# Holding the loads of partial sums and of rows of x to their place in a step, and making some weight forms a step ahead of a single-row-block step's successor

## The chip, the cores and the metric

The kernel runs on one core of a Trainium2 chip. The metric is the time of one execution on the device in microseconds (us). Before the change the median of three runs is 1437.77 us (1435.68 to 1437.93). The engines are TensorE (PE in the profile, PEld for its weight loads), VectorE (DVE), ScalarE (ACT), GpSimd (POOL) and SyncE (SP). SP does no arithmetic here: it issues DMA transfers, one after the other in the order of its queue. POOL issues DMA transfers too, and adds.

## The reference

An input x of 8 batches, 4224 tokens and 192 channels goes through a causal depthwise convolution of 7 taps (the weights are a softmax per head). Its result, called x again below, enters a token-mixing block:

```
theta = x @ w_theta
zr, zi = x * cos(theta), x * sin(theta)
y = einsum('ts,bsd->btd', w_tok_r, zr) + einsum('ts,bsd->btd', w_tok_i, zi)
u = x + y
out = u + maximum(u @ w_ch, 0)
```

The two matrices w_tok_r and w_tok_i have 4224 x 4224 elements each, so the two token products are nearly all of the work. The output is float32.

## The kernel before, in words

**Tiles.** Batches and channels together make 1536 columns. Output rows are cut into 33 row blocks of 128 tokens, input tokens into 33 chunks of 128. For each chunk a tile z of fp16 holds the products of x with cosine and sine and five sums of them. For the weights there are two staging tiles st (one for w_tok_r, one for w_tok_i), and tiles wt which hold "forms": a form is a block of weights turned into the layout that TensorE wants, or a sum or difference of two of those.

**Steps.** The token product runs in 58 steps. A step takes two row blocks (a pair) and all active chunks, at most 11. It computes a product of 2 x 2 blocks (row blocks by matrices, matrices by channel halves) with seven block products instead of eight, which is why sums of z and of weights are needed. There are 33 row blocks, so every 17th step has a single row block: steps 6, 23, 40 and 57. Such a step has four block products, uses no sums of weights, and is short. A block product over all chunks of a step is called a run below; with 11 chunks a run has 22 matmuls (L536) on accumulators y in PSUM. There are two y tiles at a time. After most runs VectorE (L461, `give`; in the first 17 steps partly ScalarE, L459) adds an accumulator into the step's partial sum pv in SBUF, and the next run on the same accumulator waits until that addition has read it.

**Partial sums.** The 33 chunks are taken in three groups of 11. So each row block is visited several times; between visits its partial sum of 768 KB lies in a DRAM tile `part`. `load_rows` (L425) loads the partial sums of the next step, and the end of `mix` (L549) stores those of this step. On some visits the rows of x themselves are added: `load_x` (L432) loads 384 KB into a tile xr, of which there is one alone, and `add_x` (L439) adds it on GpSimd. In the last visits the output is computed and stored (L585, L590).

**Forms.** `load_w` (L374, four transfers on GpSimd's queue) loads the weights of a step two steps ahead. `turn` (L387) turns a quarter of them on VectorE, and `wsum` (L399) adds or subtracts two forms. A pair step needs four turns, named "11", "21" (from w_tok_r) and "22", "12" (from w_tok_i), and four sums S1 to S4. `w_tasks` says when they are made: during the step before.

**Order.** All events of a step have a time between 0 and 7 (a seventh of the step, which in a pair step is a run). `step_events` collects them, and `mix` writes each into the program ahead of the matmul that is due. On PE, DVE and ACT, and for GpSimd's additions and weight loads, that written order is kept, by `in_order`. For DMA issues on SP no such order was asked for: a scheduler places each as soon as its buffer and data allow by its own estimate, so a load can come to stand well ahead of its event. The six buffers named "big" hold the partial sums pv and the convolution's input windows xw.

**Beside the steps.** While a group of chunks is being started (steps 0 to 5, 17 to 22, 35 to 40) TensorE also does the convolution (L216), transposes and the product with w_theta (L146) of the next step's new chunks. VectorE does four products (L297, two for each chunk) and eight sums (L306) when two new chunks start in the next step; the third sum of a chunk overwrites its x, and therefore waits for the four transfers (L263, on SP) that store that x to DRAM.

## Time and profile before

| quantity | value |
|---|---|
| median of three runs | 1437.77 us |
| the profiled execution | 1437.8 us, of which the span of the profile is 1436.0 us |
| PE busy | 1409.4 us, 98% of the span |
| DVE busy | 973.0 us, 68% |
| POOL busy | 434.3 us, 30% |
| ACT busy | 310.6 us, 22% |
| DMA | 281.99 MB, mean 196 GB/s |

The span is what the profile shows, from the first instruction of the program to the last; 1.8 us of the profiled execution's time lie around it. A line of a timeline gives the start, the length, the engine, the source line, the operation, what it writes and reads, how many instructions were merged, and in square brackets how long the engine was idle before and what ended that. "SPq" is a DMA issue on SP. Steps carry no label in the trace: they are found by counting the 7672 matmuls of L536 in order. A step has 2 matmuls for each chunk and run. By that count step 22 begins at 545.8 us, step 23 at 572.1, step 24 at 586.4, step 39 at 966.2, step 40 at 992.4, step 41 at 1010.3 and step 42 at 1038.4. In step 23 the four runs begin at 572.06, 575.63, 579.21 and 582.78 us, so a run of 22 matmuls takes 3.57 us.

### The profile page before, as it was taken

The page shows a single profiled execution, that of the slowest core. Times are in us where ns is not written, and L with a number is a line of the kernel's source. Part 1 is how long each engine was busy: PE and PEld are TensorE (multiplying, and loading weights), DVE is VectorE, ACT ScalarE, POOL GpSimd, SP SyncE. Part 2 cuts the span into 40 slices and gives each one's busy share as a digit, 9 for nine tenths or more (in the row PEclk, how much of TensorE's full clock was granted, in tenths as well). Part 3 has the DMA queues.
Part 4 walks back from the last instruction along what each step waited for, and adds up shares of the span by engine and source line. Part 5 has one row for each costly group of instructions (what it writes and reads, how often), then busy time and mean ns, then how long its engine had stood idle before and what let it go on. Part 6 is the DMA issues. An engine that isn't in the chain of part 4 may idle for free.

```text
span 1436.0 us, 23771 instructions
## 1 busy us (share of the span) xinstructions
PE 1409.4 (98%) x9829; PEld 889.7 (62%) x9829; DVE 973.0 (68%) x1046; ACT 310.6 (22%) x374; POOL 434.3 (30%) x655
## 2 busy tenths in 40 slices
PE   8889999999999999999999999999999999999997
PEld 5556666666666666666666666666566666666665
DVE  6893554545548787866665657877777677767676
ACT  5851101111124244000000004335100110010133
POOL 8511211111233332532333343233323123213110
PEclk9999999999999999999999999999999999999999
DMA  9975766564799999898899889999999999999894
GB/s 193 234 164 132 147 125 128 100 151 89 147 232 227 231 236 239 209 256 177 232 236 229 229 157 243 231 198 255 248 206 216 215 206 220 203 202 197 166 214 136
DMA packets 272045, 281.99 MB, mean 196 GB/s; under 512 B 106688, under 2 KB 240192, under 8 KB 271936
## 3 DMA queue, kind: packets, MB, share of 16 engines
q0 software_dynamic: 162464, 92.15, 48.8%
q1 hardware_dynamic: 71840, 178.88, 35.4%
q10 hardware_dynamic: 37632, 9.44, 4.5%
q8 instruction: 77, 1.26, 0.4%
q14 instruction: 32, 0.26, 0.1%
HBM read 245.49 MB, written 108.13 MB: 246 GB/s over the span
## 4 chain that ended last, share of the span: by engine, by line
PE 92%; DMA 2%; DVE 2%; ACT 1%; SPq 1%; issue 1%; POOL 0%; DVEq 0%; ACTq 0%; POOLq 0%
PE y L536 84%; PE v L146 5%; PE tp L170 1%; PE pc L216 1%; ACT z L291 1%; DMA xw<-in_x_dram 1%; DMA xw<-xw 1%; SPq L194 1%; DVE pv L461 0%; DVE z L306 0%; DVE pv L585 0%; DMA part<-pv 0%; DMA st<-in_moe_w_tok_r_dram 0%; DMA wsb<-in_weight_dram 0%; DVE wt L399 0%
## 5 line engine op out<-in xcount | busy, mean ns | idle before, releaser
L536 PE MATMUL y<-z,wt 128*128 128x384 f16 x7672 | 1282.4, 326 | 6.4 <-DVE pv L461 5.3
L536 PEld LDWEIGHTS <-wt 128*128 128x128 f16 x7672 | 743.7, 98 | 482.6 <-issue 6.3
L461 DVE TENSOR_TENSOR pv<-y,pv 128x768 f32<-128x768 f32 x317 | 302.5, 954 | 323.9 <-PE y L536 284.0
L387 DVE STREAM_TRANSPOSE wt<-st 128x1408 f16<-128x1408 f16 (+7 forms) x224 | 327.5, 1465 | 51.0 <-PE y L536 38.3
L374 POOL DMA_DIRECT2D st<-in_moe_w_tok_r_dram x232 | 132.3, 578 | 463.5 <-DVE wt L387 451.8
L374 POOL DMA_DIRECT2D st<-in_moe_w_tok_i_dram x232 | 132.4, 579 | 405.0 <-DVE wt L387 396.5
L399 DVE TENSOR_TENSOR wt<-wt 128x1408 f16<-128x1408 f16 (+6 forms) x208 | 173.4, 834 | 40.5 <-PE y L536 38.3
L156 ACT ACTIVATE z<-pc 128x768 f16<-128x768 f32 (+1 forms) x62 | 47.5, 803 | 387.0 <-PE pc L216 378.4
L156 ACT ACTIVATE ub<-pv 128x768 f16<-128x768 f32 x63 | 50.2, 836 | 343.6 <-DVE pv L461 315.9
L459 ACT ACTIVATE pv<-y 128x768 f32<-128x768 f32 x66 | 53.7, 814 | 280.5 <-PE y L536 280.5
L146 PEld LDWEIGHTS <-uT 128*128 128x128 f16 x1056 | 90.6, 98 | 23.8 <-issue 5.9
L439 POOL TENSOR_TENSOR pv<-pv,xr 128x1536 f32<-128x1536 f32 x24 | 74.5, 3103 | 66.2 <-issue 26.7
L203 POOL DMA_DIRECT2D xw<-in_x_dram x132 | 76.3, 587 | 27.1 <-issue 7.0
L585 DVE SCALAR_TENSOR_TENSOR pv<-v,pv 128x768 f32<-128x768 f32 (+1 forms) x67 | 62.8, 942 | 24.9 <-PE v L146 24.5
L306 DVE TENSOR_TENSOR z<-z 128x768 f16<-128x768 f16 x132 | 71.2, 552 | 2.2
L291 ACT ACTIVATE z<-v,half_pi 128x768 f16<-128x768 f32 x66 | 59.6, 903 | 56.4 <-PE v L146 55.7
L156 ACT ACTIVATE uT<-tp 128x1536 f16<-128x1536 f16 (+1 forms) x47 | 56.5, 1208 | 47.3 <-PE tp L170 47.3
L297 DVE TENSOR_TENSOR z<-z 128x1536 f16<-128x1536 f16 (+1 forms) x68 | 60.6, 926 | 4.3 <-ACT z L291 4.2
L146 PE MATMUL v<-wth,uT 128*128 128x192 f16 x528 | 54.4, 246 | 2.7 <-ACT z L291 2.1
L146 PE MATMUL v<-wch,uT 128*128 128x192 f16 x528 | 54.3, 246 | 1.3 <-DVE pv L585 0.7
L291 ACT ACTIVATE z<-v 128x768 f16<-128x768 f32 x66 | 53.2, 806 | 0.0
L216 PE MATMUL pc<-xw,bands 96*64 96x192 f16 x512 | 30.4, 251 | 5.4 <-DMA st<-in_moe_w_tok_r_dram 2.7
(45 smaller groups left out, 144.8 us busy)
## 6 DMA issues: line engine op xcount, KB each, us to landing
part<-pv SPq DMA_DIRECT2D x79, 768.0 KB, 4.3
pv<-part SPq DMA_DIRECT2D x79, 768.0 KB, 6.0
out_dram<-pv SPq DMA_DIRECT2D x65, 384.0 KB, 4.5
st<-in_moe_w_tok_r_dram POOLq DMA_DIRECT2D x136, 176.0 KB, 6.0
st<-in_moe_w_tok_i_dram POOLq DMA_DIRECT2D x136, 176.0 KB, 5.3
xs<-z SPq DMA_DIRECT2D x132, 96.0 KB, 5.1
xw<-in_x_dram POOLq DMA_DIRECT2D x121, 96.0 KB, 6.2
xr<-xs SPq DMA_DIRECT2D x24, 384.0 KB, 4.5
```

The source lines that it names most:

```text
L146: pe(nc.tensor.matmul(v[:, k, b * D : (b + 1) * D], lhsT=tT[:, 3 * k + b + i, :], rhs=w[:, 2 * b + i, :], start=(i == 0), stop=(i == 1),))
L156: act(nc.scalar.activation(out=out, in_=in_, func=AT.Copy))
L203: nc.gpsimd.dma_start(out=self.xw[lo : lo + n, h, :, :], in_=x[:, t0 : t0 + n, :].rearrange("b s d -> s b d"),)
L291: act(nc.scalar.activation(**args))
L306: dve(nc.vector.tensor_tensor(out=z[:, o, :], in0=z[:, a, :], in1=z[:, b, :], op=ALU.subtract))
L374: pool(nc.gpsimd.dma_start(out=st[a * Q : (a + 1) * Q, 0:nb, :, 0:n] .rearrange("i r bt s -> i (r bt) s"), in_=w[self.tbs[0] * P : (self.t ...
L387: dve(nc.vector.transpose(self.w[name][:, 0 : self.n, :, :], self.st[int(name[1])][:, int(name[0]) - 1, :, 0 : self.n * Q] .rearrange("p b ...
L399: dve(nc.vector.tensor_tensor(out=self.w[name][:, 0 : self.n, :, :], in0=self.w[a][:, 0 : self.n, :, :], in1=self.w[b][:, 0 : self.n, :, : ...
L439: ins = pool(nc.gpsimd.tensor_tensor(out=self.pv[i], in0=self.pv[i], in1=self.xr[i], op=ALU.add))
L461: dve(nc.vector.tensor_tensor(out=o, in0=yv, in1=o, op=ALU.add))
L536: pe(nc.tensor.matmul(y[cn][:, q, 0:BH], lhsT=self.w[wn][:, c, :, :].rearrange("p bt i -> p (bt i)"), rhs=chunks[k].z[:, zn, q * BH : (q + ...
L585: dve(nc.vector.scalar_tensor_tensor(out=ub[:, ks, :], in0=v[:, ks, :], scalar=0.0, in1=ub[:, ks, :], op0=ALU.max, op1=ALU.add,))
```

## The change

Three things are changed.

- Every load of partial sums and of rows of x (`load_rows`, `load_x`) now waits for the VectorE instruction that was last written into the program before it. `add_x` did so before.
- For the pair steps that follow a single-row-block step (7, 24 and 41) the forms "11", "21" and S3 are made at the end of the step two ahead (5, 22 and 39) by `early_tasks`; the rest of the forms stays in the single-row-block step (6, 23, 40) at other places.
- In a single-row-block step the two loads of weights for the step two ahead stand at 0.1 and 3.1 instead of 1.3 and 4.3.

```
+    def paced(ins):
+        tc.add_manual_dep(ins.ins, last["dve"].ins.name, SYNC, reason="pace")
+        return ins
...
+            if self.t and not steps[self.t - 1].pair:
+                return [
+                    (0.3, lambda: self.turn("22")), (1.1, lambda: self.wsum("S1")),
+                    (1.9, lambda: self.wsum("S2")), (2.9, lambda: self.turn("12")),
+                    (4.0, lambda: self.wsum("S4")),
+                ]
...
+        def early_tasks(self):
+
+            return [
+                (5.9, lambda: self.turn("11")), (6.3, lambda: self.turn("21")),
+                (6.6, lambda: self.wsum("S3")),
+            ]
...
-                    nc.sync.dma_start(
+                    paced(nc.sync.dma_start(
                         out=pv, in_=part[(self.t // NU - 1) % 2][tb, :, :]
-                    )
+                    ))
...
-            nc.sync.dma_start(
+            paced(nc.sync.dma_start(
                 out=self.xr[i], in_=xs[self.tbs[i] * P : (self.tbs[i] + 1) * P, :]
-            )
+            ))
...
-            tc.add_manual_dep(ins.ins, last["dve"].ins.name, SYNC, reason="pace")
+            paced(ins)
...
-                found.append((1.3 + 3 * (m - 1), lambda m=m: nxt.load_w(m)))
+                at = 1.3 + 3 * (m - 1) if s.pair else (0.1, 3.1)[m - 1]
+                found.append((at, lambda m=m: nxt.load_w(m)))
+            if not steps[t + 1].pair:
+                found += nxt.early_tasks()
```

The order of instructions on PE and ACT is the same in both programs. On DVE it differs at the three places around steps 5, 22 and 39. On SP and POOL, DMA issues change places in many steps; those that matter to a step of the prediction are named there.

## The prediction, made before the changed kernel was run

> **What bounds the kernel now.** I read the busy shares first, then the slices, then who waited for whom on PE from 990 us on, then timelines around the single-row-block steps. The page:

> ```profile
> PE 1409.4 (98%) x9829; PEld 889.7 (62%) x9829; DVE 973.0 (68%) x1046; ACT 310.6 (22%) x374; POOL 434.3 (30%) x655
> ...
> PE   8889999999999999999999999999999999999997
> ...
> q0 software_dynamic: 162464, 92.15, 48.8%
> q1 hardware_dynamic: 71840, 178.88, 35.4%
> ```

> TensorE is idle for 26.6 us of 1436.0, and the change leaves every matmul in place, so only idle time can be won. The slices put most of it in the start (14 us before 99 us) and the end (8 us after 1411 us), where the edits hardly reach. In between PE has no gap from 101 to 1004 us, steps 22 to 24 included; what the middle loses lies around step 40. In the waits of PE from 990 us on the largest row, and the timeline of the place (start, length, engine, line; in brackets idle time and who ended it):

> ```profile
> PE y L536 <- DVE pv L461: 3.5, 4, 1.9
> ```

> ```profile
> 996.97 2.28 POOL L374 DMA_DIRECT2D st<-in_moe_w_tok_r_dram  x4 [7.49 <-DVE wt L387]
> ...
> 1001.53 2.30 SPq L425 DMA_DIRECT2D pv<-part  x3
> ...
> 1013.97 0.95 DVE L461 TENSOR_TENSOR pv<-y,pv 128x768 f32<-128x768 f32 x1
> ...
> 1014.97 3.73 PE L536 MATMUL y<-z,wt 128*128 128x384 f16 x22 [0.90 <-DVE pv L461]
> ...
> 1018.03 1.65 DVE L387 STREAM_TRANSPOSE wt<-st 128x1408 f16<-128x1408 f16 x1 [3.11 <-DMA st<-in_moe_w_tok_r_dram]
> 1019.60 0.92 DVE L461 TENSOR_TENSOR pv<-y,pv 128x768 f32<-128x768 f32 x1
> ...
> 1020.57 24.70 PE L536 MATMUL y<-z,wt 128*128 128x384 f16 x151 [1.86 <-DVE pv L461]
> ```

> Two stalls, 0.90 + 1.86 = 2.76 us. In the first VectorE is merely behind (four forms and sums, and the products of two new chunks, in a short step). In the second it sits 3.11 us for weights issued at 997 us, because five loads of partial sums, two at 997.6 and three at 1001.5, shared the DMA engines with them: these weights took up to 19.2 us to land (the transfers of tile st from 990 to 1030 us), against a median of 6.0 on the page.

> **Part 1, the moved forms.** "11", "21" and S3 leave steps 6, 23 and 40 for steps 5, 22 and 39. VectorE before, at the end of step 22:

> ```profile
> 570.35 0.95 DVE L461 TENSOR_TENSOR pv<-y,pv 128x768 f32<-128x768 f32 x1
> 571.21 1.14 DVE L306 TENSOR_TENSOR z<-z 128x768 f16<-128x768 f16 x2
> 572.27 0.95 DVE L461 TENSOR_TENSOR pv<-y,pv 128x768 f32<-128x768 f32 x1
> 573.14 3.16 DVE L387 STREAM_TRANSPOSE wt<-st 128x1408 f16<-128x1408 f16 x2
> 576.22 0.92 DVE L461 TENSOR_TENSOR pv<-y,pv 128x768 f32<-128x768 f32 x1
> 577.06 0.87 DVE L399 TENSOR_TENSOR wt<-wt 128x1408 f16<-128x1408 f16 x1
> ```

> VectorE has no idle time there, and in the changed program's order both turns and S3 stand ahead of the addition at 572.27, the last of step 22. From starts: two turns 576.22 - 573.14 = 3.08, S3 577.86 - 577.06 = 0.80, together 3.88 us. The addition ends at 577.1. The second run of step 23 needs its accumulator at 575.63, so PE stalls 1.52 us where it had none. In step 39 the same 3.88 us put the addition of 992.64 to 996.5, ending 997.4; step 40's second run, spread out by convolution and transposes, wants it at 996.93: 0.45 us lost. In return VectorE is done in step 40 ahead of step 41's second run (1013.9 against 1014.4 by the same replay): the 0.90 goes. What is late next there: step 40's last sums, which wait for the x stores queued on SP behind the loads for step 41; these now go about 3 us later, behind an addition at 1000.6. In step 5 VectorE has 18 of 25 us free, and three late forms cost nothing; without that cover it would be 1.5 us as in step 22.

> **Part 2, the loads of step 42 and 43** leave step 40 for 1.6 sevenths into steps 41 and 42. The weights issued at 997 us (now about 996, since "21" is turned earlier) then share the engines with two loads of sums instead of five. By the page's rows q0, the weights' queue, moves 92.15 MB in 48.8% of 1436 us, 131 MB a ms, and q1 352: 5.5 us of engine time for 704 KB of weights, 2.2 for a load of sums. All that is in flight from 996.5 comes to some 13 us; VectorE wants the weights at 1013.8. The 3.11 us and the 1.86 us go. Same sum for the old order: 20 us from 997.5, which is the landing seen.

> **Part 3, the loads of step 24.** This is where I expect the price.

> ```profile
> 557.50 1.49 SPq L425 DMA_DIRECT2D pv<-part  x3
> ...
> 581.43 3.10 POOL L439 TENSOR_TENSOR pv<-pv,xr 128x1536 f32<-128x1536 f32 x1 [2.56 <-DVE wt L399]
> ...
> 584.56 0.32 SPq L432 DMA_DIRECT2D xr<-xs  x1
> ...
> 589.38 3.10 POOL L439 TENSOR_TENSOR pv<-pv,xr 128x1536 f32<-128x1536 f32 x1 [2.60 <-DMA xr<-xs]
> ...
> 594.89 0.32 SPq L425 DMA_DIRECT2D pv<-part  x1
> 595.31 0.37 SPq L432 DMA_DIRECT2D xr<-xs  x1
> ```

> Step 24 is the first that adds x. Before, its sums came at 557.5, and the first rows of x had been in their tile since 70 us; even so the second addition of x ended at 592.5, 1.3 us ahead of VectorE's addition of 593.78. Now both sums wait for the first addition of step 23, which ends at 580.5, and the rows of x, third in SP's queue, for S2 at 581.3. GpSimd's queue has the second load of weights ahead of x's addition; it needs "12" (582.8), so the queue is free at 585.2 and does not decide. The second rows need the single tile xr, and SP now has the store of step 23's sum ahead of them, issued by 589: it does not decide either.

> When do the first rows land? Nearest row: the rows issued at 595.31 behind one load of sums, with weights beside, landed 9.0 us on. One more load ahead is 2.2: 581.3 + 11.2 = 592.5. Ends: 589.1 (three loads at 557.50 took 9.6 us together; 580.5 + 9.6 less 1.0 for the half-size third) and 596 (everything shared evenly with both loads of weights, by the engine times of part 2). From there: addition of x 3.1, VectorE 0.95, 0.1 for semaphores: step 24's third run can start at 596.65, and wants to at 595.0 (586.4 + 1.5 + 2 x 3.57): 1.65 us. The second rows: 0.1, a lone load 3.0 (that issued at 607.6 took 2.9), addition 3.1, and 1.1 to PE's release: 7.3 us after the first addition of x, against 1.05 + 3.57 until the fourth run wants it: 2.7 us more. Together 4.4 us; 0.9 at the early end, 7.9 at the late.

> [...]

> **The other held loads.** In steps 25 to 35 and 44 to 57 a load now starts 1.6 sevenths into the step before, often 10 to 25 us later. Landing and both additions of x take at most 12 + 3.1 + 4.6 + 3.1 = 23 us; run 4 of the next step needs them 30 us on: hidden, with some 7 us in hand. In steps 17 to 22 and 36 to 39 most loads stood within 2 us of their new place already. The tail's last load goes from 1397.5 to about 1407, lands 6 us later, and is used at 1423.

> **Sum.** -0.90 - 1.86 + 0.45 + 1.52 + 4.4 = +3.6 us on the profiled execution's 1437.8 (span 1436.0 and 1.8 around it), which equals the median: 1441.4 us, 0.25% slower. With the ends of part 3: 1437.9 to 1444.9. About 0.2%, 2.9 us, is what a measurement tells from no change.

> **Rivals.**
> - *Not slower*: the three loads before step 24 land by 589. Then step 24 costs 0.9 us or less and the sum is -0.8 to +0.1: 1437.0 to 1437.9. For it: 557.5 us. Against: no weights were landing then. It decides at 590.9, where the third run stops stalling. 0.20.
> - *Faster*: VectorE's order costs less than replayed (steps 23, 40 and 24 all free), and 2.76 to 3.0 us are won: 1434.9. Against: no idle time in its rows. 0.08.
> - *The old wait comes back*: weights or x stores still late in step 41, 1.9 us: 1443.3. For it: the loads for step 41 still run beside them. 0.10.
> - *x late in later steps*, as with step 24, in steps 25 to 52: 2 to 3 us in two of them, 1446. Against: the 7 us. 0.06.

> **How the numbers follow.** My forecast has 0.56; about a fifth of it lies within 2.9 us. Slower: 0.45 + 0.10 + 0.06 = 0.61; same: 0.11 + 0.20 = 0.31; faster 0.08. Leaving out the faster case and the top, the range is 1437.0 to 1445.5.

> **What would show it.** Right: no PE gap at 1014 to 1021 us; a gap of about 1.5 us at the second run of step 23, one of 0.5 at that of step 40, two gaps totalling 3 to 6 us at the third and fourth run of step 24, ended by VectorE, which waits for GpSimd. Wrong: VectorE idle before step 22's last addition, rows of x landed by 589, or PE gaps between 600 and 990 us or in the steps after 42.

## The result, and the profile after

The changed kernel took 1442.92 us (median of 19 runs, 1438.84 to 1459.18) against 1436.95 us before (19 runs): +6.0 us by the medians, a ratio of 1.0046 with a 95% interval of 1.0033 to 1.0059. It is slower, by 0.46%. The forecast was 1441.4 us with a range of 1437.0 to 1445.5.

The profiled execution took 1443.42 us (span 1441.3). First the page, then the waits of PE from 90 to 1420 us (engine and line, what it waited for, total us, times, longest):

```profile
PE 1412.0 (98%) x9829; PEld 890.8 (62%) x9829; DVE 970.5 (67%) x1046; ACT 310.6 (22%) x374; POOL 434.0 (30%) x655
```

```profile
PE y L553 <- DVE pv L478: 7.9, 5, 2.6
PE pc L220 <- DMA xw<-in_x_dram: 0.4, 2, 0.2
```

The row that held 5.3 us before holds 7.9. Another part of the lost time is in no wait: PE is busy for 1412.0 us instead of 1409.4 with the same matmuls, because it ran some of them at half of its clock: from 71.54 to 78.37 us the granted clock was 0.50 and PE busy for 5.01 us with 30 matmuls, against 6.83 us with 71 in the next 6.83 us at 1.00. Where the waits lie is in the timeline of PE, steps 22 to 25 and then 40 to 41:

```profile
569.78 7.96 PE L553 MATMUL y<-z,wt 128*128 128x384 f16 x48
579.24 18.04 PE L553 MATMUL y<-z,wt 128*128 128x384 f16 x110 [1.49 <-DVE pv L478]
598.89 3.73 PE L553 MATMUL y<-z,wt 128*128 128x384 f16 x22 [1.62 <-DVE pv L478]
605.24 6.99 PE L553 MATMUL y<-z,wt 128*128 128x384 f16 x42 [2.62 <-DVE pv L478]
```

```profile
1005.84 0.81 PE L553 MATMUL y<-z,wt 128*128 128x384 f16 x4 [0.38 <-DVE pv L478]
...
1016.00 29.25 PE L553 MATMUL y<-z,wt 128*128 128x384 f16 x179
```

So the two stalls of step 41 are gone: its matmuls now run in one piece. In their place stand 1.49 us in step 23 (forecast 1.52), 1.62 and 2.62 in step 24 (forecast 1.65 and 2.7) and 0.38 in step 40 (forecast 0.45). VectorE at the end of step 22 shows the first of them; all of it without a pause:

```profile
573.17 1.64 DVE L391 STREAM_TRANSPOSE wt<-st 128x1408 f16<-128x1408 f16 x1
574.73 1.11 DVE L310 TENSOR_TENSOR z<-z 128x768 f16<-128x768 f16 x2
575.75 1.64 DVE L391 STREAM_TRANSPOSE wt<-st 128x1408 f16<-128x1408 f16 x1
577.42 0.89 DVE L403 TENSOR_TENSOR wt<-wt 128x1408 f16<-128x1408 f16 x1
578.23 0.95 DVE L478 TENSOR_TENSOR pv<-y,pv 128x768 f32<-128x768 f32 x1
...
597.88 0.96 DVE L478 TENSOR_TENSOR pv<-y,pv 128x768 f32<-128x768 f32 x1 [5.21 <-POOL pv L456]
...
604.23 0.96 DVE L478 TENSOR_TENSOR pv<-y,pv 128x768 f32<-128x768 f32 x1 [3.84 <-POOL pv L456]
```

Two turns and S3 stand ahead of the addition of 578.23, the last of step 22, and PE starts again at 579.24 when it is done. The lower two lines are the stalls of step 24: VectorE waits 5.21 and 3.84 us for GpSimd's additions of x. Those, with SP's issues, in the timeline of all engines:

```profile
582.56 1.10 SPq L442 DMA_DIRECT2D pv<-part  x2
583.75 0.39 SPq L449 DMA_DIRECT2D xr<-xs  x1
...
585.18 2.28 POOL L378 DMA_DIRECT2D st<-in_moe_w_tok_i_dram  x4 [5.21 <-DVE wt L391]
...
594.75 3.10 POOL L456 TENSOR_TENSOR pv<-pv,xr 128x1536 f32<-128x1536 f32 x1 [7.29 <-DMA xr<-xs]
597.87 0.32 SPq L449 DMA_DIRECT2D xr<-xs  x1
...
601.10 3.10 POOL L456 TENSOR_TENSOR pv<-pv,xr 128x1536 f32<-128x1536 f32 x1 [3.26 <-DMA xr<-xs]
```

The rows of x go out at 583.75 as third in the queue and hold GpSimd until 594.75; the second rows go out only at 597.87, when the first have been added.

Steps can be laid side by side by the start of each in the two traces (counted in matmuls). A gap costs about 0.16 us more than it shows (1.65 for a gap of 1.49): the record of a matmul is 0.33 us long and the next one normally starts 0.16 us into it, which it cannot do across a gap. Us gained (-) or lost by the step, against the trace of before:

| kernel | 23 | 24 | 40 | 41 | the four | median against before |
|---|---|---|---|---|---|---|
| changed | 1.65 | 4.56 | 0.54 | -3.08 | +3.7 | +6.0 |
| changed, second profile (e12) | 1.65 | 5.25 | 0.54 | -1.81 | +5.6 | |
| e1 forms only | 1.65 | 8.07 | 0.55 | -3.08 | +7.2 | +6.7 |
| e2 hold only | 0 | 11.73 | 0 | -1.95 | +9.8 | +11.4 |
| e3 no hold on 24 | 1.63 | 0 | 0.54 | -2.08 | +0.1 | +0.9 |
| e4 forms for 41 | 0 | 5.67 | 0.54 | -3.08 | +3.1 | +5.1 |
| e5 hold, not on 24 | 0 | 0 | 0 | -1.95 | -2.0 | -0.9 |
| e6 hold, not on 24, forms for 41 | 0 | 0.35 | 0.54 | -2.83 | -1.9 | -0.3 |
| e7 hold and weight places | 0 | 5.11 | 0 | -1.96 | +3.2 | +6.9 |
| e8 forms, hold 25 and 26 | 1.64 | 0 | 0.54 | -3.08 | -0.9 | -0.8 |
| e9 forms for 41 alone | 0 | 0 | 0.55 | -3.08 | -2.5 | -1.7 |
| e10 the same, S3 late | 0 | 0 | 0.01 | -1.81 | -1.8 | -2.8 |
| e11 sums of 24 free | 1.64 | 0 | 0.55 | -3.08 | -0.9 | +1.9 |

The five columns of steps are of one profiled execution each, the last column is of all runs; e1 to e4, e5 to e8 and e9 to e11 shared their runs of before (1437.31, 1436.84 and 1437.39 us). Outside the four steps the first profile of the changed kernel lost 1.5 us in the start and 0.46 us in step 20, where PE waits for a window of the input; the second lost 1.75 us in the start and 1.0 us in step 18, with 0.77 us of such a wait.

### The profile page after: what moved, and what is told of

Same layout as the page of the kernel before. It is cut to its first block, busy times and chain, and to the rows that moved or that the text cites. A ratio compares the mean times of both kernels' runs of the same rounds, so it can differ in the third digit from the quotient of the medians.

```text
span 1441.3 us, 23794 instructions
## 1 busy us (share of the span) xinstructions
PE 1412.0 (98%) x9829; PEld 890.8 (62%) x9829; DVE 970.5 (67%) x1046; ACT 310.6 (22%) x374; POOL 434.0 (30%) x655
## 3 DMA queue, kind: packets, MB, share of 16 engines
q0 software_dynamic: 162464, 92.15, 48.1%
q1 hardware_dynamic: 71840, 178.88, 34.7%
## 4 chain that ended last, share of the span: by engine, by line
PE 86%; DMA 5%; DVE 5%; ACT 2%; issue 1%; POOL 1%; SPq 0%; DVEq 0%; ACTq 0%; POOLq 0%
PE y L553 78%; PE v L150 5%; DMA xw<-in_x_dram 2%; DVE wt L391 1%; PE tp L174 1%; DVE pv L478 1%; PE pc L220 1%; ACT z L295 1%; DMA st<-in_moe_w_tok_r_dram 1%; DMA xr<-xs 1%; DMA xw<-xw 1%; DVE z L310 1%; DVE z L301 1%; POOL st L378 1%; POOL pv L456 0%
## 5 line engine op out<-in xcount | busy, mean ns | idle before, releaser
L553 PEld LDWEIGHTS <-wt 128*128 128x128 f16 x7672 | 743.9, 98 | 486.7 <-issue 10.9
L602 DVE SCALAR_TENSOR_TENSOR pv<-v,pv 128x768 f32<-128x768 f32 (+1 forms) x67 | 62.9, 942 | 24.9 <-PE v L150 24.5
```

Of the source, the lines that this page charges most:

```text
L553: pe(nc.tensor.matmul(y[cn][:, q, 0:BH], lhsT=self.w[wn][:, c, :, :].rearrange("p bt i -> p (bt i)"), rhs=chunks[k].z[:, zn, q * BH : (q + ...
```

## Experiments: the parts alone

Theory A is the prediction's: stalls of the middle add up. Theory B puts what lies beyond this sum to the start, where the first rows of x are no longer loaded at 70 us; theory C to chance dips of the clock. The first four take the parts of the change one at a time.

**e1, the forms alone.** From the changed kernel:

```
-                    paced(nc.sync.dma_start(
+                    ins = nc.sync.dma_start(
...
-            paced(nc.sync.dma_start(
+            ins = nc.sync.dma_start(
```

> Only the forms (and the places of the weight loads) are moved; no load of sums or of x is held. Theory A (the stalls of the middle add up, each costing its gap and about 0.16 us): step 23 loses 1.65 us and step 40 0.54, the first stall of step 41 (1.06) goes, its second stays at 1.9 within 1 us because the five loads at 997 us are back, and steps 24 has no stall: +1.1 us, some 1438. Theory B (what the changed kernel lost beyond the sum of its middle, about 2 to 3 us, comes from the start, where the first rows of x are no longer loaded at 70 us): here that load is back, so the granted clock is 0.999 or 1.0 in nearly all executions. Theory C (the start's clock dips by chance of each execution, whatever the edit): clocks of 0.995 to 0.998 in many executions here too, and a time 2 us higher.

Measured: 1444.05 us, ratio 1.0048 (1.0035 to 1.0061), 6 us over the expectation. Steps 23, 40 and 41 came out as theory A had them (the second stall of step 41 left as well), but step 24, where no load is held, lost 8.07 us: one stall of 5.67 us in its fourth run, and half clock behind it. PE, SP's queue and then GpSimd's in this run, and what SP's issues waited for from 578 to 600 us:

```profile
603.56 8.75 PE L553 MATMUL y<-z,wt 128*128 128x384 f16 x39 [5.67 <-DVE pv L478]
```

```profile
585.53 0.32 SPq L442 DMA_DIRECT2D pv<-part  x1
588.19 0.32 SPq L566 DMA_DIRECT2D part<-pv  x1
594.21 0.32 SPq L442 DMA_DIRECT2D pv<-part  x1
594.62 8.24 SPq L449 DMA_DIRECT2D xr<-xs  x2
```

```profile
584.52 3.10 POOL L456 TENSOR_TENSOR pv<-pv,xr 128x1536 f32<-128x1536 f32 x1
599.43 3.09 POOL L456 TENSOR_TENSOR pv<-pv,xr 128x1536 f32<-128x1536 f32 x1 [11.81 <-DMA xr<-xs]
```

```profile
SPq L442 <- DMA part<-pv: 14.5, 2, 8.9
```

The tile xr is free at 587.6, but the second rows of x go out at 594.62, 7.0 us later, behind the two loads of sums for step 26 (585.53 and 594.21), which wait 14.5 us in all until stores have emptied their buffers. In the kernel before, the same rows went out at 584.56, ahead of the second of those loads (594.89). The moved forms and weight loads put the first addition of x later on GpSimd; that the order of SP's queue changed because of this is likely but not shown.

**e2, the hold alone.** From the changed kernel:

```
-            if self.t and not steps[self.t - 1].pair:
+            if False:
...
-                at = 1.3 + 3 * (m - 1) if s.pair else (0.1, 3.1)[m - 1]
+                at = 1.3 + 3 * (m - 1)
...
-            if not steps[t + 1].pair:
+            if False:
                 found += nxt.early_tasks()
```

> Only the loads of sums and of x are held; the forms and the weight loads stand as before. Theory A: two stalls in step 24 together of 4.4 us (4.57 with the lost overlaps) as in the changed kernel, no stall in step 23, the second stall of step 41 (2.0) gone, its first (0.9) still there or smaller: +2.6 us, some 1439.5. Theory B adds 2 to 3 us with clocks below 0.999 in most executions: 1442. Rival on step 24: if the moved forms, not the hold, make its x late, step 24 stalls by less than 2 us here and the time is 1437 or less.

Measured: 1448.68 us, 1.0080 (1.0067 to 1.0094): the hold alone is dearer than the whole change. Step 23 is free of stalls and the 1.9 us of step 41 are gone, both as expected. In step 24 PE stalls 2.47 and 5.05 us, in its fourth and fifth run. PE, GpSimd, then VectorE:

```profile
600.07 5.42 PE L553 MATMUL y<-z,wt 128*128 128x384 f16 x22 [2.47 <-DVE pv L478]
610.53 5.78 PE L553 MATMUL y<-z,wt 128*128 128x384 f16 x21 [5.05 <-DVE pv L478]
```

```profile
588.77 3.10 POOL L456 TENSOR_TENSOR pv<-pv,xr 128x1536 f32<-128x1536 f32 x1 [9.55 <-DMA xr<-xs]
591.82 2.30 POOL L378 DMA_DIRECT2D st<-in_moe_w_tok_i_dram  x4
```

```profile
607.99 1.65 DVE L391 STREAM_TRANSPOSE wt<-st 128x1408 f16<-128x1408 f16 x1 [7.18 <-DMA st<-in_moe_w_tok_i_dram]
```

GpSimd stands 9.55 us for the held rows of x, and the weights for step 25 stand behind it in its queue. They go out at 591.82 (before: 584.48), and VectorE then sits 7.18 us for them, with the additions that free PE's accumulators behind. In the changed kernel the new places of the weight loads put them ahead of that addition (585.18).

**e3, the changed kernel without the hold on step 24.**

```
+                    if self.t != 24:
+                        paced(ins)
...
+            if self.t != 24:
+                paced(ins)
```

> The changed kernel, but the loads of step 24 (both sums and both rows of x) are not held and go to their old places; everything else as changed. Theory A: no stall in step 24, steps 23 and 40 lose 1.65 and 0.54, both stalls of step 41 gone: -0.9 us, some 1436. Theory B: the clock of the start recovers too, 0.999 or 1.0 in nearly all executions. Theory C: clocks still scattered from 0.995 to 1.0, time near 1438. If the step 24 stalls come from another cause, 4 us stay: 1440 or more.

Measured: 1438.25 us, 1.0010 (0.9999 to 1.0021). Step 24 has no stall; 5.0 us of the 6.0 came back. In step 41 a stall of 0.84 us returned: VectorE waited 1.39 us for x stores. The mean granted clock was 0.998 or more in all 12 runs, against 8 of 19 in the changed kernel.

**e4, early forms for step 41 alone, all loads held.**

```
-            if self.t and not steps[self.t - 1].pair:
+            if self.t == 41:
...
-            if not steps[t + 1].pair:
+            if (t + 2) == 41:
                 found += nxt.early_tasks()
```

> The changed kernel, but only step 41 has its forms made early (those of steps 7 and 24 stand where they were); all loads held. Theory A: the 1.65 us of step 23 go; TensorE reaches step 24 that much earlier while its rows of x come no earlier, so step 24 may stall longer by up to the same 1.65: +2.0 to +3.7 us, 1439 to 1440.7 with the start as before. Theory B: clocks as in the changed kernel (0.994 to 1.0, most at 0.997), 2 us more.

Measured: 1442.42 us, 1.0038 (1.0020 to 1.0055). The 1.65 us of step 23 went and step 24 lost 5.67 instead of 4.56, of which 3.83 is one gap and 1.7 half clock behind it. The rows of x came earlier, too: counted from the start of step 23, GpSimd adds the first 17.1 us on (20.7 in the changed kernel), and the third run no longer stalls; it adds the second 24.9 us on (27.1), still too late for the fourth run. So the gaps cost a little less than in the changed kernel, 4.0 us instead of 4.56, and the slow clock made them dearer.

## Experiments: one queue at a time

Theory A2 is what e1 to e4 left: each stall of step 24 is a transfer behind another in a queue, and its own hold is only one way to it.

**e5, the hold alone, but not on step 24** (e2 with the two conditions of e3):

> Only the loads are held, and not those of step 24; forms and weight loads as before. Theory A2 (what the first runs left standing: each stall of step 24 is one queue behind another, the hold of its own loads being one cause, and the second stall of step 41 goes with the hold of the loads for 42 and 43): no stall in steps 23 and 24, the 0.90 of step 41 still there or smaller, the 1.86 gone: -1.1 to -2.0 us, 1435.3 to 1436.2, clocks as before the change. Rival (the hold of any later load delays step 24 too): 3 us or more in step 24, 1439 or above.

Measured: 1435.93 us, 1.0001 (0.9990 to 1.0012). No stall in steps 23 and 24, 1.95 us won in step 41, 0.97 us left there: theory A2 by the trace. In the median 0.9 us, which the interval does not tell from no change.

**e6, the same with early forms for step 41** (e3 and e4 together):

> The changed kernel without the hold on step 24's loads and with early forms for step 41 alone (weight loads at their new places). Theory A2: the 1.65 us of step 23 go as well, no stall in step 24; step 40 loses 0.54; step 41 has between nothing and 0.85 (the x stores landed just in time in the changed kernel and 0.8 late in the run that left step 24's loads free): -1.5 to -2.5 us, 1434.8 to 1435.8. Rival (the gain of the middle is taken back by the start, whose stalls are longer when TensorE comes earlier): nothing is gained, 1437.

Measured: 1436.51 us, 1.0005 (0.9987 to 1.0023), 12 runs from 1434.4 to 1448.3. The trace has the -1.9 us, with a stall of 0.18 us in step 24, where none was expected; the runs are too far apart to show them. In the profiled execution the start took nothing back (step 23 begins 0.06 us earlier than before); for the other runs this stays open.

**e7, e2 with the new places of the weight loads:**

```
-                at = 1.3 + 3 * (m - 1)
+                at = 1.3 + 3 * (m - 1) if s.pair else (0.1, 3.1)[m - 1]
```

> All loads held as in the changed kernel and the weight loads of the single-row-block steps at their new places, but no early forms. In the run with the hold alone, the fifth run of step 24 stalled 5.05 us. Theory A2 (that is GpSimd's queue: the second weights for step 25 go out behind the addition of x, which waits for the held rows): with the weights ahead of the addition this stall is gone, what is left in step 24 is 2.5 to 5 us of late rows of x, and a slow clock after it in some executions: 1440 to 1443. Rival (VectorE is behind, not the weights): the 5 us stay, 1447 or more.

Measured: 1443.69 us, 1.0046 (1.0032 to 1.0061), 4.5 us better than e2 when each is taken against its own runs of before: the stall of the fifth run is gone, one of 3.27 us stays in the fourth. The 5.05 us were GpSimd's queue.

**e8, e1 with the loads for steps 25 and 26 held:**

```
+                    if self.t in (25, 26):
+                        paced(ins)
...
+            if self.t in (25, 26):
+                paced(ins)
```

> The early forms and new places of the weight loads, with only the loads for steps 25 and 26 held. In the run of the forms alone the fourth run of step 24 stalled 5.67 us, and the second rows of x stood on SP's queue behind loads of sums for step 26 that waited for a buffer. Theory A2 (head of line): with those loads behind the rows of x the 5.67 us and the slow clock after it (2.2 us) go; step 23 still loses 1.65, step 40 0.54, step 41 gains 1.06 and perhaps the rest: 1437 to 1438.5. Rival (the late addition of x on GpSimd, 3 to 4 us behind its old time, is enough by itself): 3 us or more stay in step 24, 1441 or above.

Measured: 1436.06 us, 0.9994 (0.9985 to 1.0003), 7.5 us better than e1 in the same way. With those loads behind the rows of x step 24 has no stall, so it was the queue. The first addition of x begins 13.5 us after the start of step 23 in both e1 and e8, so its being later costs nothing by itself.

**e9 and e10, step 41 alone.** The kernel before, with early forms for step 41 and the new weight places in step 40 only; e10 leaves S3 in step 40.

```
+            if self.t == 41:
...
+                at = (0.1, 3.1)[m - 1] if t == 40 else 1.3 + 3 * (m - 1)
...
+            if (t + 2) == 41:
+                found += nxt.early_tasks()
```

> The kernel before with one thing of the change: step 41's two turns and S3 made in step 39 and the weight loads of step 40 at their new places; no load held, steps 5 to 24 as before. Theory A2 with what the run of the forms alone showed (both stalls of step 41 go without any hold): -3.1 us in step 41, +0.5 in step 40, nothing else: -2.5 us, 1434.4. Rival (the hold of the loads for 42 and 43 is needed, and what the forms-only run gained was due to its other moves): the 1.9 stays, -0.5 us, 1436.4.

> As the one with step 41's forms alone, but S3 stays in step 40. Theory A2: VectorE has 0.8 us less ahead of step 39's last addition, so the 0.54 of step 40 goes; it has 0.8 us more ahead of step 40's last sums, and the first stall of step 41 returns in part, 0 to 0.5: -2.5 to -3.1 us, 1433.8 to 1434.4. Rival (step 41 has no slack for it): its stall is back at 0.9 or more, 1435 or above.

Measured: e9 1435.68 us, 0.9993 (0.9982 to 1.0005); e10 1434.56 us, 0.9982 (0.9969 to 0.9995). Both stalls of step 41 go in e9 with no load held. Counted from the start of step 40, the loads of sums moved in SP's queue: one of the two for step 41 goes out 5.5 us earlier, those for step 42 at 12.9 instead of 9.1 us, and the first for step 43 at 21.9 instead of 11.1. The weights for step 42 go out 1.1 us earlier, and their last transfer lands 17.1 us after the start of the step instead of 25.5. Early forms and early weight loads were not tried one without the other here. In e10 step 40 loses 0.01 instead of 0.54 and the first stall of step 41 does not return. A later one does, in the timeline of PE:

```profile
1007.32 17.71 PE L553 MATMUL y<-z,wt 128*128 128x384 f16 x108
1026.14 19.17 PE L553 MATMUL y<-z,wt 128*128 128x384 f16 x117 [1.11 <-DVE pv L478]
```

VectorE waited 3.93 us ahead of a turn at 1023.60; the last of the four weight transfers for that turn landed at 1023.5. e10 is faster than the kernel before by 2.8 us in the median (0.7 to 4.5 by the interval). Its four steps won less than those of e9, 1.8 against 2.5 us, and the intervals of the two overlap, so which of them is better is open. Holding the loads for steps 42 and 43 in it as well was not tried.

**e11, the changed kernel with the sums of step 24 free, its rows of x held:**

```
+                    if self.t != 24:
+                        paced(ins)
```

> The changed kernel with the sums of step 24 not held; its rows of x and all other loads held. Theory A2 (the rows of x were late because they stood third behind two loads of sums that shared the engines with them): alone on the queue at 583.5 they land by 588.5, about when GpSimd is free of the weight loads, and step 24 has no stall: -0.9 us, 1436 to 1438. Rival (the hold on the rows of x alone is enough to make them late, weights being in flight): 2 us or more in step 24, 1440 or above. Theory B once more (without the early load of x the start is slower): clocks at 0.997 or less in most executions.

Measured: in the trace the rows of x, alone on the queue, go out at 580.91 and GpSimd adds them at 585.95; step 24 has no stall, as theory A2 has it. But the time is 1439.24 us, 1.0022 (1.0007 to 1.0036), 11 runs from 1436.6 to 1446.8, and the profiled execution is the fastest of them: its -0.9 us is not typical. What the other runs lost is not shown.

**e12, the changed kernel profiled once more:**

> The changed kernel unedited, a second profiled execution. Theory D (the 2 us or so that the median of the changed kernel lies above the sum of its stalls come from executions in which the rows of x for step 24 land a little later, the stall there is 3 us or longer and the clock falls to one half behind it): the stalls of steps 23 and 40 come out at 1.49 and 0.38 again to within 0.05, since VectorE's order alone sets them; those of step 24 differ from 1.62 and 2.62 by half a microsecond or more, and if one of them is over 3 us a stretch of slow clock follows it and step 24 loses 1.5 us or more beyond the gaps. Theory C (only the start is slow, by chance): the gaps of step 24 are the same again and the clock behind them is 1.00.

Measured (one execution): 1445.91 us. Steps 23 and 40 stall 1.49 and 0.38 us again, to the last digit. Step 24 stalls 0.93 and 2.54 us, and loses 5.25 us, because the clock fell. Windows of 2 us (start and end, length, PE busy and its instructions, granted clock, share of the DMA engines, GB/s), this execution first, the other second:

```profile
602.00:604.00 2.00, 0.94 (x6) 1.00 0.90 356
604.00:606.00 2.00, 0.51 (x2) 0.76 0.91 376
606.00:608.00 2.00, 2.00 (x7) 0.50 0.97 136
608.00:610.00 2.00, 2.00 (x12) 0.88 1.12 265
```

```profile
604.00:606.00 2.00, 0.76 (x5) 1.00 0.92 361
606.00:608.00 2.00, 2.00 (x14) 1.00 0.96 128
```

With PE busy throughout, 7 matmuls were done in 2 us instead of 14. The 3 us of theory D are wrong: 2.54 us were enough here. Of its two stalls one differs by the half microsecond that it asked for (0.93 against 1.62), the other does not. Step 41, too, had a stall this time, 1.10 us; VectorE waited 1.65 us for x stores:

```profile
1023.23 1.15 DVE L310 TENSOR_TENSOR z<-z 128x768 f16<-128x768 f16 x2 [1.65 <-DMA xs<-z]
```

## Why the prediction was right, and where it was not

- **Direction and size.** Forecast +3.6 us for the profiled execution; the four steps it named lost 3.7. The median moved by 6.0. The sum was right for the steps; the other 2.3 us of the median are in none of its terms.
- **Moved forms.** 1.52 us in step 23 and 0.45 in step 40, both priced from 3.88 us of VectorE rows, measured 1.49 and 0.38 in both profiles of the changed kernel. e4 and e5, without early forms for step 24, have no stall in step 23.
- **Rows of x of step 24.** Forecast: landing 11.2 us after issue, stalls of 1.65 and 2.7 us. Measured: the rows landed 10.9 us after the issue, stalls of 1.62 and 2.62 us. The landing by 589 us of the rival "Not slower" did not come: the three loads took 12.1 us together, from 582.56 to 594.67 us, with weights in flight beside them. e3 shows the hold as the cause inside the changed kernel, and e11 that it is the held sums ahead of the rows: alone on the queue these landed in 5.0 us. The range of 0.9 to 7.9 us was wide for good reason: e12, e4 and e7 have one stall or two, from 0.9 to 3.8 us.
- **"The 3.11 us and the 1.86 us go"** was right, but the step gave it to the hold. e1 and e9 hold nothing there and lose both stalls; e2, e5 and e7 hold, without the moved forms, and lose the second. Either is enough, since either takes loads of sums out of the time in which the weights for step 42 land: the last of these lands 17.1 (e9) and 18.0 us (e5) after the start of step 40, before the change 25.5. The prediction's order of VectorE had the moved forms in it, yet it followed SP's queue only for the held loads.
- **The parts one at a time** would have been mispriced: +1.1 us was expected of the forms alone (e1), +6.7 measured; +2.6 of the hold alone (e2), +11.4 measured. That GpSimd's queue "does not decide" holds for the whole change only. In e1 the rows of x stood behind two loads that waited for buffers, in e2 the waiting addition held the weights. The hold on steps 25 and 26 covers the first, the new weight places the second, and the forecast, which read GpSimd's queue rightly for the whole change, named neither as a cover. That each part's price was covered by another is luck as far as the forecast goes.
- **The term that was missing** is the clock. The sum priced each stall at its length. In e12, 3.5 us of gaps in step 24 cost 5.25 us, in e1 5.67 us cost 8.07, in e2 7.5 us cost 11.7. The mean clock was 0.997 or less in 32 of 42 runs of the kernels whose profile has a stall of 1 us or more in step 24 (all 16 of e1, e2 and e7, 11 of 19 of the changed kernel, 5 of 7 of e4), in 24 of 83 runs of the others (none of 12 in e3, but 5 of 12 in e6 and e9 and 6 of 12 in e10), and in 26 of 76 runs of the kernel before beside the experiments. So it is not only step 24. The first profile of the changed kernel fell back by 3.1 us near 73 us, with a gap of 3.47 us (2.31 before) and 6.8 us of half clock, and came out of the start 1.5 us late. e9, which has the loads of the kernel before there, fell back by 2.55 us at the same place, with half clock from 72.8 to 79.6 us. Theory C fits the start, theory D part of step 24.
- **The old wait coming back** (1.9 us, 0.10) looks like too low a chance: x stores were just in time in the first profile and late in e12 (1.10 us) and e3 (0.84 us).
- **Theory B is not borne out.** Without the early load of x the longest stall near 73 us was 0.5 to 3.5 us in six profiles, with it 1.1 to 2.6 us in eight, and the start came out -0.9 to +1.8 us late without it and -1.7 to +2.1 with it. A difference below 1 us is not excluded. Yet kernels that hold step 24's rows of x lie 1.6 to 3.7 us above the sum of their four steps (changed, e2, e4, e7, e11) and the others -1.0 to +1.6. e12 shows some 2 us of it as step 24 and step 41 of a worse execution; for e11, where the profile has no stall, the cause stays open.
- **Early or late.** Each is worth something at one place: leaving the loads of step 24 early 5.0 us (e3), holding the later ones, those for steps 42 and 43 among them, 1.95 us in step 41 (e5).

## What to carry to other kernels

A load that is held can free the engines for others (in e5 the last of the weights for step 42 landed 18.0 us after the start of step 40, before the change 25.5), but its price is set where it is first used: find the first user whose load used to be far ahead and do the sum there, as for step 24. Before a part of a change is called harmless, see what it moves ahead of or behind what else in the same queue; here the parts alone cost 7 and 11 us and together 6, since each covered a blocked queue that another had opened. And where TensorE is the bound, a stall can cost more than its length: behind gaps of 2.54 us (e12) and 5.67 us (e1) half clock took another 1.5 and 2.2 us, behind one of 2.62 us (changed) nothing.

## What the hardware showed that was not expected

```profile
600.00:601.00 1.00, 0.83 (x3) 0.64 0.63 38
601.00:602.00 1.00, 1.00 (x5) 0.50 1.19 171
602.00:603.00 1.00, 1.00 (x5) 0.50 1.27 252
603.00:604.00 1.00, 1.00 (x6) 0.66 1.10 343
```

0.64 is half clock for 0.72 us, 0.66 for 0.68: 3.4 us together, and half of that, 1.7 us, is what step 24 lost there beyond its gap (5.67 - 3.83 - 0.16 = 1.68). In the four short drops PE stood idle for at most 0.44 us (e12); in the two long ones it was idle for the first 2.2 us (e1) and 2.3 us (e2).

The trace records when the granted clock changes: in the first profile of the changed kernel at 13.52, 71.54, 78.37 and 1440.29 us, the drop between them being 6.83 us long, and in that of the kernel before at 14.12 and 1434.06 us. From 90 to 1430 us neither shows half clock.

The length of a gap alone did not set the clock in these runs. Behind the gap of 2.62 us in step 24 (changed, from 602.62 to 605.24 us) it stayed at 1.00, behind that of 2.54 us in e12 it fell. Nor did the busy time in 3.41 us, the length of a short drop: PE was busy for 0.79 us of them in the changed kernel and for 1.55 us in the kernel before, with the two stalls of step 41, and the clock stayed; it was busy for 1.30 us in e12 in the stretch that ended where the clock fell. The changed kernel, then e12, then the kernel before (columns as above):

```profile
602.00:605.41 3.41, 0.79 (x6) 1.00 0.97 404
605.41:608.82 3.41, 3.41 (x23) 1.00 0.95 183
```

```profile
601.64:605.05 3.41, 1.30 (x9) 1.00 0.98 364
605.05:608.46 3.41, 2.97 (x10) 0.50 0.94 211
```

```profile
1017.63:1021.04 3.41, 1.55 (x10) 1.00 0.63 231
1021.04:1024.45 3.41, 3.41 (x23) 1.00 0.45 120
```

What set e12 apart from the first profile is not shown by these rows.

In the two profiles of the changed kernel the stalls that VectorE's order alone sets were the same to the last digit (1.49 and 0.38 us); what hangs on a landing was not (0.93 against 1.62 us in step 24, no stall against 1.10 us in step 41).
